# The first token block computed in two column halves, with the early transfers spread over other queues

## The chip, the cores and the metric

The kernel runs on one core of a Trainium2 chip. The metric is the device time of one execution in microseconds (us). The engines of a core work side by side, each through its own list of instructions in order, and wait for each other by semaphores: TensorE (PE in the profile; PEld is its weight load), VectorE (DVE), ScalarE (ACT), GpSimd (POOL) and SyncE (SP), which here only issues transfers. The two transfers' rings that matter are the hardware ring of SyncE and the software ring of GpSimd.

## The reference

Two layers, one behind the other: a causal convolution along the sequence, with one softmaxed filter of 7 taps for each of 8 heads of 24 channels, and a feed-forward layer with the exact GELU.

```python
# x: (8, 4096, 192) f32, weight: (8, 7)
w = softmax(weight, axis=-1)
x_pad = concat([zeros((B, 6, D)), x], axis=1)
x_unf = x_pad[:, idx, :].reshape(B, S, K, H, group)
y = einsum('hk,bskhg->bshg', w, x_unf).reshape(B * S, D)
# w_in: (192, 2048), w_out: (2048, 192), y: (32768, 192)
h = y @ w_in
g = 0.5 * h * (1.0 + erf(h / sqrt(2)))
return g @ w_out
```

## The kernel before

The 32768 tokens are two halves of 16384 that are worked on at the same time: one on partitions 0 to 63, the other on partitions 64 to 127. A half is cut into blocks n of WS[n] token columns, six of 256 and then 29 of 512. The 192 channels are three thirds p of 64. W_in's 2048 columns are 16 chunks of 128.

For each block the x load brings token rows into `xin` (four transfers, L252 to L265), VectorE transposes them into `xT`, a third at a time (`trans`, L465), GpSimd adds the six columns that come from the block before (`halo`, L344), the convolution gives `xc` in bf16, TensorE multiplies W_in with `xc` into PSUM (`mm1`, L659), ScalarE takes the GELU of 1024 columns a time into `gT` (L612), and TensorE multiplies with W_out (`mm2`, L693, for the blocks of 256 and the last one, `mm2_t`, L728, for the others). The results are evacuated and stored by SyncE.

The convolution of most blocks is done on VectorE (`conv`, L487: a tensor_scalar and six scalar_tensor_tensor a third). The first two blocks (`PC`, L34) have theirs on TensorE (`pconv`, L627): `xT` is cast to bf16 (`xTb`), and for each third and tap two 64x64 diagonal matrices `dg` (made by `diag`, L427, a third at a time) multiply shifted columns of it, 14 matmuls a third. The sum lands in one PSUM bank a third (`CONVB`, L166) and is copied to `xc`: for block 0 by ScalarE (cast at L572, copy at L579), for block 1 by VectorE (`cast`, L452, `conv_out`, L459).

TensorE's order at the start is: 16 warm-up matmuls (L625), the 42 convolution matmuls of block 0, then mm1(0,i) for the slices i = 0 to 7. A slice is two chunks by 256 columns, 12 matmuls, and fills one of the two PSUM buffers `hp`; slice i waits until GELU i-2 has emptied it. Behind slices 4, 5 and 6 comes one third each of block 1's convolution (`behind`, L655). Then mm1(1,0), and from there mm1(1,i) with pieces of mm2(0) between, the first of which waits for W_out (L782).

W_in comes in three parts (`win_in`, columns 0:256, 256:512, 512:1024 of each half, L322), and each partition half needs the other's columns too: VectorE copies them across (`dup`, L435, two copies a part). mm1(0,0), (0,2) and (0,4) wait for the parts 0, 1 and 2 and their copies (L669).

The order on VectorE at the start (L523 to L536) is diag(0), diag(1), trans(0,0..2), diag(2), dup(0..2), trans(1,0..2), cast(1,0..2), and then block 2's operations, with conv_out(1,0..2) put between them. GpSimd's (L379 to L390) is halo(0), six x loads (two of block 1, four of block 2, named in `SW`, L131), the W_out transfer, halo(1), four x loads of block 3, then the halos of the other blocks. SyncE has the first two loads of block 0, waits for W_in's first part, has the other two of block 1, waits for block 3's loads (L799), and goes on with block 4; ScalarE issues the other two loads of block 0.

Of the kernel before, what the change touches and what calls it, by code (L numbers as in the profile page):

```python
# [11 lines left out]
def bass_lightweight_conv__then__act_gelu_exact_kernel(  # L12
# [7 lines left out]
    B, SEQ, D = x.shape  # L20
# [12 lines left out]
    WS = [256] * 6 + [512] * ((HALF - 1536) // 512)  # L33
    PC = {0: 0, 1: 1}  # L34

    NA = 6
# [67 lines left out]
    with es:  # L104
# [24 lines left out]


        SW = {1: (2, 3), 2: (0, 2, 1, 3), 3: (0, 2, 1, 3)}  # L131

        S_WSB = sem("S_WSB")
        S_WIN = [sem("S_WIN%d" % i) for i in range(3)]
        S_WOUT = sem("S_WOUT")
        S_XG = {n: sem("S_XG%d" % n) for n in SW}
        S_XIN = [sem("S_XIN%d" % i) for i in range(NX)]
# [7 lines left out]
        S_HOT = sem("S_HOT")  # L145
        S_CAST = [sem("S_CAST%d" % i) for i in range(len(PC))]
        S_PC = sem("S_PC")
# [16 lines left out]


        CONVB = {0: [0, 1, 2], 1: [3, 0, 1]}  # L166

        NCV = NP * KS
# [7 lines left out]

        def pce(n, p):

            return NP * PC[n] + p + 1

# [9 lines left out]
        def xin_at(n):  # L190

            return sum(64 - 16 * len(SW.get(m, ())) for m in range(n % NX, n + 1, NX))

# [15 lines left out]
        def wait_banks(t, m, g):  # L209

            k = G0[m] + g
            if m < M0:
                if k >= 2:
                    t.wait_ge(S_EVA, k - 1)
            else:
                e = k - G0[M1]
                t.wait_ge(S_EV, EVC[M1] + (-2 if e == 0 else e - 1))

        def evac(e, m, g):
# [32 lines left out]
        def load(e, n, qs=(0, 2, 1, 3), sm=None):  # L252
            mb = WS[n] // 32
            if n >= NX:
                e.wait_ge(S_TR, NP * (n - NX + 1))
            for q in qs:
                off = ((q // 2) * HALF + OFF[n]) * D + DQ * (q % 2)
                e.dma_start(  # L258
                    ap(
                        xin[n % NX],  # L260
                        32 * q * (TB // 32 * DQ),
                        [[TB // 32 * DQ, 32], [DQ, mb], [1, DQ]],
                    ),
                    ap(xt, off, [[mb * D, 32], [D, mb], [1, DQ]]),
                ).then_inc(sm or S_XIN[n % NX], 16)  # L265
# [55 lines left out]
        def _(g):  # L321
# [22 lines left out]
            def halo(n):  # L344
# [3 lines left out]
                if n >= 2 and n not in PC:  # L348
                    if n - 2 in PC:
                        g.wait_ge(S_PCE, pce(n - 2, NP - 1))  # L350
                    else:
                        g.wait_ge(S_CV, cvd(n - 2))
# [27 lines left out]
            halo(0)  # L380
            load(g, 1, SW[1], S_XG[1])
            load(g, 2, SW[2], S_XG[2])
            g.dma_start(
# [3 lines left out]
            halo(1)  # L387
            load(g, 3, SW[3], S_XG[3])
            for n in range(2, NB):
# [3 lines left out]
        def _(v):  # L393
# [57 lines left out]

            def cast(n, p):  # L452
                v.wait_ge(S_TR, NP * n + p + 1)
                v.tensor_copy(
                    ap(xTb[PC[n]], p * XB + HL, [[NP * XB, 128], [1, WS[n]]]),
                    ap(xT[n % 2], p * XW + HL, [[NP * XW, 128], [1, WS[n]]]),
                ).then_inc(S_CAST[PC[n]])

            def conv_out(n, p):  # L459
                v.wait_ge(S_PC, pce(n, p))  # L460
                v.tensor_copy(  # L461
                    xc[n % 2][:, p * TB : p * TB + WS[n]], bank(CONVB[n][p], w=WS[n])
                ).then_inc(S_PCE)

            def trans(n, p):  # L465
                w = WS[n]
                if p == 0:
                    if xin_at(n) > 0:
                        v.wait_ge(S_XIN[n % NX], xin_at(n))
                    if n in SW:  # L470
                        v.wait_ge(S_XG[n], 16 * len(SW[n]))
                    if n >= 2 and n - 2 in PC:
                        v.wait_ge(S_PCE, pce(n - 2, NP - 1))
                    elif n >= 2:
                        v.wait_ge(S_CV, cvd(n - 2))
                    if n >= 1:
                        v.wait_ge(S_HALO, HC[n])
                v.transpose(  # L478
                    ap(xT[n % 2], p * XW + HL, [[NP * XW, 128], [1, w]]),
                    ap(  # L480
                        xin[n % NX],
                        p,
                        [[TB // 32 * DQ, 128], [DQ, w // 32], [NP, 32]],
                    ),
                ).then_inc(S_TR)
# [36 lines left out]

            diag(0)  # L523
            diag(1)
            for p in range(NP):
                trans(0, p)
            diag(2)
            dup(0)
            dup(1)
            dup(2)  # L530
            for p in range(NP):
                trans(1, p)
            for p in range(NP):
                cast(1, p)

            side = [((2, (0, 3, 5)[p]), conv_out, 1, p) for p in range(NP)]  # L536
            for n in range(M0, M1):
# [18 lines left out]
        def _(a):  # L556
# [12 lines left out]
            a.activation(out=hot[:, 1:2], in_=warm[0:1, 0:1], func=AF.Gelu).then_inc(S_HOT)  # L569
            for p in range(NP):  # L570
                a.wait_ge(S_TR, p + 1)
                a.activation(  # L572
                    out=ap(xTb[0], p * XB + HL, [[NP * XB, 128], [1, WS[0]]]),
                    in_=ap(xT[0], p * XW + HL, [[NP * XW, 128], [1, WS[0]]]),
                    func=AF.Copy,
                ).then_inc(S_CAST[0])
            for p in range(NP):
                a.wait_ge(S_PC, p + 1)
                a.activation(  # L579
                    out=xc[0][:, p * TB : p * TB + WS[0]],  # L580
                    in_=bank(CONVB[0][p], w=WS[0]),
                    func=AF.Copy,
                ).then_inc(S_PCE)

            due = {(1, 6): [(0, 0)]}
# [4 lines left out]
            for n in range(NB):  # L590
                w = WS[n]
                for i in range(NSL[n]):
# [5 lines left out]
                    if i == 0 and n >= 2:  # L598
                        a.wait_ge(S_MM2, MMC[n - 1])
                    if M0 <= n < M1:  # L600

# [6 lines left out]
                    else:  # L608
# [3 lines left out]
                    a.activation(  # L612
                        out=ap(gT[n % 2], i * c * 2 * w, dst),
                        in_=ap(hp[u % 2], 0, src),
# [7 lines left out]
        def _(t):  # L622
# [3 lines left out]

            def pconv(n, p, k):  # L627

                w = WS[n]
                if k == KS - 1:  # L630
                    t.wait_ge(S_CAST[PC[n]], p + 1)
                    if n == 0:
                        t.wait_ge(S_DG, p + 1)
                if k == KS - 2:
                    t.wait_ge(S_HALO, HC[n] + 2 + p)
                for hf in range(2):
                    r = slice(64 * hf, 64 * hf + 64)
                    d0 = (p * KS + k) * 64
                    x0 = p * XB + 32 * k
                    ins = t.matmul(  # L640
                        bank(CONVB[n][p], r, w),
                        dg[r, d0 : d0 + 64],
# [7 lines left out]

            taps = [(p, k) for p in range(NP) for k in range(KS - 1, -1, -1)]
            for p, k in taps:
                pconv(0, p, k)

            behind = {}  # L655
            for p in range(NP):
                behind[0, 4 + p] = [(1, p, k) for k in range(KS - 1, -1, -1)]

            def mm1(n, i):  # L659
                w, c = WS[n], NCH[n]  # L660
                u = SL0[n] + i
                if u >= 2:
                    t.wait_ge(S_GELU, u - 1)
                if i == 0:
                    if n in PC:
                        t.wait_ge(S_PCE, pce(n, NP - 2))
                    else:
                        t.wait_ge(S_CV, cvd(n))
                if n == 0 and i in (0, 2, 4):  # L669
                    t.wait_ge(S_WIN[i // 2], 32)  # L670
                    t.wait_ge(S_DUPE, 2 * (i // 2) + 2)
                for cc in range(c):
                    f0 = 128 * CH[i * c + cc]
                    for p in range(NP):
                        if n in PC and i == 0 and cc == 0 and p == NP - 1:
                            t.wait_ge(S_PCE, pce(n, p))
                        for hf in range(2):
                            r = slice(64 * hf, 64 * hf + 64)
                            fw = 64 if M0 < n <= M1 else 128
                            for fo in range(0, 128, fw):  # L680
# [4 lines left out]
                                    win[r, f1 : f1 + fw],  # L685
                                    xc[n % 2][r, p * TB : p * TB + w],
                                    start=(p == 0),
# [5 lines left out]
            def mm2(m, g, ph, i):  # L693
# [4 lines left out]
                if i == 0:  # L698
                    if ph == 0:
                        wait_banks(t, m, g)  # L700
                    else:
                        t.wait_ge(S_PH, PHC[m] + g + 1)
                if g == 0 and ph == 0:

                    c = NCH[m]
                    if i % max(c, 8) == 0:
                        last = min(NF, i + max(c, 8))
                        t.wait_ge(S_GELU, SL0[m] + last // c)
# [63 lines left out]
            for n in range(NB):  # L772
                todo = units(n - 1) if n >= 1 else []
                for i in range(NSL[n]):
                    mm1(n, i)
                    for q in behind.get((n, i), []):
                        pconv(*q)
# [16 lines left out]
        def _(sp):  # L794
            sp.dma_start(wsb[:, :], ap(wt, 0, [[KS, H], [1, KS]])).then_inc(S_WSB, 16)
            load(sp, 0, (0, 1))
            sp.wait_ge(S_WIN[0], 32)
            load(sp, 1, (0, 1))
            sp.wait_ge(S_XG[3], 64)  # L799
            for n in range(1, NB):  # L800
# [35 lines left out]
```

## Time and profile before

| | |
|---|---|
| time, median of 6 executions | 686.46 us (685.98 to 687.57) |
| the profiled execution | 685.98 us, of which the span from first to last instruction is 684.2 us |
| granted TensorE clock | 1.00 |
| matmuls mm1 (L683) | 6048, 418.6 us busy |
| matmuls mm2_t (L747) and mm2 (L714) | 5376, 366.4 us, and 1024, 52.2 us |
| convolution matmuls (L640) | 84, 5.3 us |
| GELU (L612) | 512, 1023 ns each |
| convolution on VectorE (L508, L501) | 594 and 99 instructions, 435.3 us |
| W_out transfer | issued by GpSimd at 12.22 us, 768 KB, 8.5 us to landing |

Busy times of TensorE overlap: two matmuls on different halves of the array run at once, so the sum of the groups is above the span. A line of the chain of waits says when a piece began, how long it held up the chain, and what it was; a line of the timeline gives start, length, engine, source line, operation, tiles and count, and in brackets what the engine idled for just before. All times start from the span's first instruction.

### The profile page before, as it was taken

Reading aid. Unit: us, or ns where it says so; the run is one execution under the profiler, and the core shown is the slowest. Engines: PE = TensorE matmul, PEld = TensorE weight load, DVE = VectorE, ACT = ScalarE, POOL = GpSimd, SP = SyncE. Lnnn points to the kernel's source line nnn. Section 1 sums busy time; section 2 is a strip of 40 time slices with the busy share of each in tenths; the row PEclk is TensorE's granted clock in tenths of the full one; section 3 lists DMA queues with packets and bytes.
Section 4 is the critical chain, followed back from the end, with each engine's and each line's share of the span. In section 5 each row is a group of like instructions: output and inputs, shape, how many; then the busy total and the mean of one; then the engine's idle time right before and its main releaser. Section 6 shows DMA issues by size and latency. Waiting matters only on the chain.

```text
span 684.2 us, 27314 instructions
## 1 busy us (share of the span) xinstructions
PE 677.5 (99%) x12548; PEld 409.2 (60%) x12548; DVE 580.6 (85%) x914; ACT 532.1 (78%) x536; POOL 45.6 (7%) x97
## 2 busy tenths in 40 slices
PE   8999999999999999999999999999999999999997
PEld 4899655555555555555555555555555555555556
DVE  7999989888899888898888898888898888998702
ACT  6788987777787777777877778777778777877771
POOL 8110000000000000000000000000000000000000
PEclk9999999999999999999999999999999999999999
DMA  8444521244432344422344422444323444221224
GB/s 137 93 110 97 116 61 36 61 95 95 94 69 50 74 94 95 94 53 56 84 94 95 87 53 53 93 94 94 72 56 65 95 94 95 59 56 30 48 49 94
DMA packets 133234, 53.66 MB, mean 78 GB/s; under 512 B 127552, under 2 KB 132960, under 8 KB 133120
## 3 DMA queue, kind: packets, MB, share of 16 engines
q1 hardware_dynamic: 128144, 48.78, 33.6%
q0 software_dynamic: 3792, 2.56, 2.5%
q8 instruction: 98, 1.61, 1.0%
q10 hardware_dynamic: 1184, 0.59, 0.3%
q14 instruction: 16, 0.13, 0.1%
HBM read 28.31 MB, written 25.17 MB: 78 GB/s over the span
## 4 chain that ended last, share of the span: by engine, by line
PE 96%; ACT 2%; DVE 1%; issue 0%; ACTq 0%
PE hp L683 47%; PE ob L747 42%; PE ob L714 5%; ACT gT L612 2%; PE ob L640 1%; DVE dg L428 0%; ACT L558 0%; ACT osb L227 0%; DVE wcol L420 0%; DVE osb L247 0%; DVE osb L229 0%; DVE xT L478 0%; ACT xTb L572 0%; ACT wex L562 0%; ACT xc L579 0%
## 5 line engine op out<-in xcount | busy, mean ns | idle before, releaser
L612 ACT ACTIVATE gT<-hp 128x1024 bf16<-128x1024 f32 x512 | 522.9, 1023 | 133.2 <-PE hp L683 130.0
L683 PE MATMUL hp<-xc,win 64*64 64x512 bf16 (+2 forms) x6048 | 418.6, 366 | 1.0 <-ACT gT L612 0.7
L747 PE MATMUL ob<-gT,wout 64*64 64x512 bf16 x5376 | 366.4, 376 | 0.0
L508 DVE SCALAR_TENSOR_TENSOR acc<-xT,wcol,acc 128x512 f32<-128x512 f32 (+1 forms) x495 | 314.2, 698 | 0.0
L683 PEld LDWEIGHTS hp<-xc,win 64*64 64x64 bf16 (+1 forms) x6048 | 187.8, 106 | 135.6 <-ACT gT L612 2.1
L747 PEld LDWEIGHTS ob<-gT,wout 64*64 64x64 bf16 x5376 | 172.2, 118 | 122.9
L247 DVE STREAM_TRANSPOSE osb<-ob 128x512 f32<-128x512 f32 x84 | 73.8, 881 | 86.9 <-PE ob L747 86.9
L478 DVE STREAM_TRANSPOSE xT<-xin 128x512 f32<-128x512 f32 (+1 forms) x105 | 78.3, 797 | 0.0
L508 DVE SCALAR_TENSOR_TENSOR xc<-xT,wcol,acc 128x512 bf16<-128x512 f32 (+1 forms) x99 | 65.0, 710 | 0.0
L374 POOL COPY xT<-xT 128x558 f32<-128x558 f32 x33 | 21.5, 652 | 578.9 <-DVE xT L478 578.9
L501 DVE TENSOR_SCALAR acc<-xT,wcol 128x512 f32<-128x512 f32 (+1 forms) x99 | 56.1, 618 | 1.1
L714 PE MATMUL ob<-wout,gT 64*128 64x192 bf16 x1024 | 52.2, 243 | 0.3
L714 PEld LDWEIGHTS ob<-wout,gT 64*128 64x128 bf16 x1024 | 43.6, 94 | 6.4 <-PE ob L714 0.6
L357 POOL COPY xT<-xT 128x18 f32<-128x18 f32 x30 | 11.6, 386 | 1.4 <-DVE xc L461 1.4
L229 DVE COPY osb<-ob 128x384 f32<-128x384 f32 x4 | 2.2, 557 | 7.8 <-PE ob L714 7.8
L625 PE MATMUL hp<-warm 128*128 128x512 bf16 x16 | 5.9, 547 | 1.3 <-DVE warm L394 1.3
L640 PE MATMUL ob<-xTb,dg 64*64 64x256 bf16 x84 | 5.3, 272 | 0.7 <-ACT xTb L572 0.7
L227 ACT ACTIVATE osb<-ob 128x384 f32<-128x384 f32 x12 | 5.8, 486 | 0.0
L258 POOL DMA_DIRECT2D xin<-in_x_dram x10 | 5.8, 587 | 0.0
L640 PEld LDWEIGHTS ob<-xTb,dg 64*64 64x64 bf16 x84 | 4.3, 107 | 1.8 <-ACT xTb L572 1.2
L625 PEld LDWEIGHTS hp<-warm 128*128 128x128 bf16 x16 | 2.0, 132 | 4.6 <-issue 3.0
L324 POOL DMA_DIRECT2D win<-in_moe_w_in_dram x6 | 3.9, 651 | 0.0
(32 smaller groups left out, 21.8 us busy)
## 6 DMA issues: line engine op xcount, KB each, us to landing
xin<-in_x_dram SPq DMA_DIRECT2D x116, 192.0 KB, 4.5
out_dram<-osb SPq DMA_DIRECT2D x112, 192.0 KB, 3.6
out_dram<-osb SPq DMA_DIRECT2D x56, 48.0 KB, 1.7
xin<-in_x_dram SPq DMA_DIRECT2D x12, 96.0 KB, 3.0
xin<-in_x_dram POOLq DMA_DIRECT2D x10, 96.0 KB, 2.9
wout<-in_moe_w_out_dram POOLq DMA_DIRECT2D x1, 768.0 KB, 8.5
win<-in_moe_w_in_dram POOLq DMA_DIRECT2D x4, 96.0 KB, 3.9
win<-in_moe_w_in_dram POOLq DMA_DIRECT2D x2, 192.0 KB, 5.2
```

The source lines that it names most:

```text
L247: v.transpose(ap(osb[m % 2], j, [[8 * C, 128], [C // 2, TB // 32], [NP, 32]]), bank(ring(m, j)),).then_inc(S_EV)
L357: g.tensor_copy(dst, ap(xT[(n - 1) % 2], WS[n - 1] + 31, [[NP * XW, 128], [XW, NP], [32, HB]],),).then_inc(S_HALO)
L374: g.tensor_copy(ap(t, 1, [[NP * tw, 128], [tw, NP], [32, HB], [1, 31]]), ap(t, WS[n], [[NP * tw, 128], [tw, NP], [32, HB], [1, 31]]),).the ...
L478: v.transpose(ap(xT[n % 2], p * XW + HL, [[NP * XW, 128], [1, w]]), ap(xin[n % NX], p, [[TB // 32 * DQ, 128], [DQ, w // 32], [NP, 32]],),) ...
L501: ins = v.tensor_scalar(a, src, wk, None, ALU.mult)
L508: ins = v.scalar_tensor_tensor(dst, src, wk, a, op0=ALU.mult, op1=ALU.add)
L612: a.activation(out=ap(gT[n % 2], i * c * 2 * w, dst), in_=ap(hp[u % 2], 0, src), func=AF.Gelu,).then_inc(S_GELU)
L625: t.matmul(hp[1][:, 0:512], warm[:, 0:128], warm[:, :])
L640: ins = t.matmul(bank(CONVB[n][p], r, w), dg[r, d0 : d0 + 64], xTb[PC[n]][r, x0 : x0 + w], start=(k == KS - 1), stop=(k == 0), tile_positi ...
L683: ins = t.matmul(hp[u % 2][fo : fo + fw, o : o + w], win[r, f1 : f1 + fw], xc[n % 2][r, p * TB : p * TB + w], start=(p == 0), stop=(p == N ...
L714: ins = t.matmul(bank(bb[sub], w=C), gT[m % 2][r, c0 : c0 + 128], wout[r, CH[i] * C : (CH[i] + 1) * C], start=(ph == 0 and i == 0), stop=( ...
L747: ins = t.matmul(bank(ring(m, j), slice(64 * h, 64 * h + 64), w), ap(wout, 64 * hf * NF * C + CH[i] * C + j, [[NF * C, 64], [NP, 64]],), g ...
```

## The change

Block 0's convolution becomes two parts of 128 columns each, and block 1's a third (`PARTS`: block, first column, width, PSUM banks). TensorE does part 0, mm1(0,0), part 1 (`behind[0]`), mm1(0,1) and so on. For block 0 the slices 0 to 3 cover the chunks 0 to 7 in another way: four chunks by 128 columns, 24 matmuls a slice, slices 0 and 1 for the first columns and 2 and 3 for the second; slices 4 to 7 stay as they were. So mm1(0,0) needs W_in's part 0 and its copies, mm1(0,1) part 1, mm1(0,4) part 2. ScalarE writes the GELU of slices 0 to 3 to matching places of `gT`.

```diff
+    PARTS = [(0, 0, 128, (0, 1, 2)), (0, 128, 128, (3, 0, 1)), (1, 0, 256, (2, 3, 0))]
...
+            behind = {
+                0: third(1, 0) + third(1, 1) + third(1, 2),
+                4: third(2, 0),
+                5: third(2, 1),
+                6: third(2, 2),
+            }
...
+                part = {(0, 0): 0, (0, 2): 1, (1, 0): 2}.get((n, i))
+                if part is not None:
+                    t.wait_ge(S_PCE, pce(part, NP - 2))
...
+                if n == 0 and i < 4:
+                    w, c = 128, 4
+                    x0, ci = i // 2 * w, i % 2 * c
+                if n == 0 and i in (0, 1, 4):
+                    k = min(i, 2)
+                    t.wait_ge(S_WIN[k], 32)
+                    t.wait_ge(S_DUPE, 2 * k + 2)
```

The casts of part 0 are ScalarE's, those of part 1 GpSimd's, those of part 2 VectorE's; the copies to `xc` are ScalarE's for part 0 and VectorE's for the others. The third diagonal matrix set, diag(2) on VectorE before, is made by ScalarE in seven pieces of 64 columns. VectorE's order:

```diff
             diag(0)
+            trans(0, 0)
             diag(1)
-            for p in range(NP):
-                trans(0, p)
-            diag(2)
+            trans(0, 1)
+            trans(0, 2)
             dup(0)
             dup(1)
+            for p in range(NP):
+                conv_out(1, p)
             dup(2)
             for p in range(NP):
                 trans(1, p)
             for p in range(NP):
-                cast(1, p)
+                cast(v, 2, p)
```

ScalarE's:

```diff
+            a.wait_ge(S_PRO, 10)
+            a.wait_ge(S_IDN, 2)
+            for k in range(KS):
+                d0 = ((NP - 1) * KS + k) * 64
+                c0 = (NP - 1) * 32 + k
+                a.activation(
+                    out=dg[:, d0 : d0 + 64],
+                    in_=idb[:, :],
+                    func=AF.Copy,
+                    scale=wcol[:, c0 : c0 + 1],
+                ).then_inc(S_DGA)
...
+            cast0(0)
+            cast0(1)
+            conv_out0(0)
+            cast0(2)
+            conv_out0(1)
+            conv_out0(2)
```

Block 0's x load takes one run of 1440 elements a partition (eight rows of 192 less the last half row) in place of eight runs of 96, and the transposes of block 0 step over the half rows that are not wanted. GpSimd issues no x loads any more; its W_out transfer comes right behind its three casts:

```diff
             halo(0)
-            load(g, 1, SW[1], S_XG[1])
-            load(g, 2, SW[2], S_XG[2])
+            for p in range(NP):
+                cast(g, 1, p)
             g.dma_start(
                 ap(wout, 0, [[NF * C, 128], [C, NF], [1, C]]),
                 ap(woutt, 0, [[C, 128], [128 * C, NF], [1, C]]),
             ).then_inc(S_WOUT, 16)
             halo(1)
-            load(g, 3, SW[3], S_XG[3])
...
             sp.wait_ge(S_WIN[0], 32)
-            load(sp, 1, (0, 1))
-            sp.wait_ge(S_XG[3], 64)
+            load(sp, 1)
+            sp.wait_ge(S_WIN[2], 32)
+            load(sp, 2)
+            sp.wait_ge(S_WOUT, 16)
+            load(sp, 3)
```

The first pass of mm2(0) waits for the GELU of its chunks in smaller steps:

```diff
-                if g == 0 and ph == 0:
+                if m == 0:
+                    if g == 0 and ph == 0 and (i == 0 or i >= 8) and i % 2 == 0:
+                        t.wait_ge(S_GELU, max(4, i // 2 + 1))
+                elif g == 0 and ph == 0:
```

## The prediction

> **What bounds the kernel now.** I read four views, in this order: the page's busy times and its chain, to see which engine sets the end; the chain of waits over the first 60 us, since all edits lie there; the timeline of VectorE over the same stretch, since three of the edits rearrange that queue; and the groups by shape for durations.
>
> The page first: each engine's busy time, then the chain's shares.
>
> ```profile
> PE 677.5 (99%) x12548; PEld 409.2 (60%) x12548; DVE 580.6 (85%) x914; ACT 532.1 (78%) x536; POOL 45.6 (7%) x97
> PE 96%; ACT 2%; DVE 1%; issue 0%; ACTq 0%
> ```
>
> TensorE (PE) is the whole chain but for 4%, about 27 us, nearly all before the first 15 us and after 669 us. So a change to the ramp is worth what it shifts the moment from which TensorE is never again idle, one for one. The chain of waits over the first 60 us (start, length, what) shows that moment:
>
> ```profile
> 5.68 1.16 DVE dg L428 x2
> 6.84 0.45 DVE xT L478
> 7.31 0.43 ACT xTb L572
> ...
> 7.78 2.50 PE ob L640 x42
> 10.30 0.39 ACT xc L579
> ...
> 10.74 0.63 PE hp L683 x8
> 11.40 1.94 ACT gT L612 x2
> 13.35 1.03 ACT gT L612
> ...
> 14.42 0.83 PE hp L683 x12
> 15.25 0.88 PE ob L640 x14
> 16.13 0.76 PE hp L683 x12
> ```
>
> Two filter matrices, a transpose, a cast, 42 convolution matmuls, a copy, then GELUs 0 to 2 set the pace; from mm1(0,4) at 14.42 all is PE. Some 670 us follow. So the question is when mm1(0,4), and the work right behind it, starts in the new order. VectorE's timeline in the same stretch (start, length; in brackets what it idled for):
>
> ```profile
> 8.63 3.66 DVE L439 COPY win<-win 64x768 bf16<-64x768 bf16 x6
> 12.34 1.35 DVE L478 STREAM_TRANSPOSE xT<-xin 128x256 f32<-128x256 f32 x3
> 13.61 1.29 DVE L454 CAST xTb<-xT 128x256 bf16<-128x256 f32 x3
> 16.18 0.42 DVE L461 CAST xc<-ob 128x256 bf16<-128x256 f32 x1 [1.28 <-PE ob L640]
> 19.46 0.42 DVE L461 CAST xc<-ob 128x256 bf16<-128x256 f32 x1 [0.50 <-PE ob L640]
> ```
>
> The block-1 cast begins at 13.61 and TensorE takes up block 1's convolution at 15.18: VectorE has only some 0.8 us in hand there (the first cast is done 0.75 after its start, at 14.36). After 19.46 VectorE runs without idling until past 92 us; its last pieces of block 6 (from 70.59, 2.06 long) end at 72.67, and TensorE's first matmul of block 6 starts at 73.24. That is a second near-critical chain with 0.57 us of slack: TensorE can't gain more than that unless VectorE's 19.46 moves too.
>
> **The change part by part.**
>
> *x load of block 0 and the third filter matrix.* The load has one run of 1440 elements a partition instead of 8 of 96. Before, its last piece landed at about 6.7, with VectorE's second diag ending at 6.84 anyway. New order on VectorE: diag(0) from 5.68, pitch 0.54 (start to start; half of 1.16, less overlap), so trans(0,0) can start at 6.22 if the load is there, diag(1) at 6.62, trans(0,1) at 7.16, trans(0,2) at 7.58, end 8.07. But ScalarE now does seven 128x64 pieces of the third matrix first, from 5.68. No row has the shape. Bounds: from below the columns alone (GELU 1023 ns for 1024 columns against 417 for a 256-column cast is 0.79 ns a column, 0.05 us a piece, 0.35 in all); from above the 8x7 exponential with a per-partition operand, 298 ns, plus 57 columns, 0.346 a piece, 2.4 in all. Successive GELUs start 0.10 sooner than the one before ends, so I take 0.346 - 0.10 = 0.25, 1.75 in all: cast 0 starts at 7.43 instead of 7.31, and 128 columns take 417 - 101 = 0.32. First convolution matmul: 7.78, as before. **The earlier x and the moved diag bring nothing there**; if the load lands as late as before, 0.06 is lost further on. The longer runs carry 0.34 MB more, beside W_in: at the 168 GB/s of the stretch from 10 to 20 us that is 2.0 us if W_in had to wait for all of it. Its three parts landed at 6.7, 8.8 and 10.8 and are now wanted at 8.1, 9.1 and 12.2; 2.0 late, the second would hold VectorE up by 1.7 and push dup(2) by some 0.5. The other bound is nothing, as the longer runs also need an eighth of the descriptors; I take nothing.
>
> *Half-width convolution, W_in halves.* The chain gives 16 matmuls of 192 columns in 0.66 us and 12 of 256 in 0.66, two running side by side: 82 and 109 ns a pair. The line through both gives 55.5 ns at 128 columns, 0.39 per third (seven pairs). No 128-column row exists: bounds 54.5 (half of 256) and 82 (the nearest row); I take the line, since the 512-column rows (216 ns) lie on it. Third p0 runs 7.78 to about 8.17, p1 straight on; ScalarE then evacuates p0 before it casts p2 (8.58 to 8.9), so p2 runs 8.94 to 9.33, its evacuation (0.28) ends 9.86, and mm1(0,0) has its last third at 9.9 instead of 10.74. Ten pairs are left, 0.56; GELU 0 starts near 10.65 instead of 11.40. **A lead of 0.75 us.**
>
> *Part 1 behind mm1(0,0).* 42 more matmuls, 21 pairs, 1.17 us, and two changes between 64x64 and 64x128 tiles. In the trace each such change makes the start-to-start gap 0.20 instead of 0.11, so 0.09 each. mm1(0,1) goes from about 10.4 + 1.17 + 0.18 to 11.78, its 12 pairs take 0.67, and GELU 1 starts at 12.67; ScalarE idled 1.0 for it. Before, GELU 1 was at 12.32. **The lead is gone, and 0.35 more.** GELU 2 then goes at 13.6 (13.35), mm1(0,4) at 14.65 to 14.7: 0.28 late.
>
> *VectorE.* It now waits for part 1's three thirds (evacuations of 0.29 to 0.30 us at 11.1, 11.5, 11.9) before dup(2), which had started at 10.79. dup(2) then runs 12.23 to 13.78 at its old 1.55, trans(1) follows at 13.78 instead of 12.34, the cast at 15.04 instead of 13.61, part 2's first third at 15.83 instead of 15.18: 0.65, some 0.7 with the gaps behind it. Against that, the old dup(2) ran while GpSimd issued transfers, and it won't now. The cast row shows what company costs: 277 ns for the last, 743 for the first, which ran beside GpSimd's copies. At three quarters of 1.55 the shift falls to 0.33, where mm1(0,4) decides anyway. I take the middle, **+0.5 us**. VectorE's chain of later blocks moves by the same, so its slack of 0.57 holds.
>
> *Queues.* GpSimd gives up ten x loads (0.58 each to issue) and takes three 128x128 casts after its halo copies; its 186-column cast takes 0.34, so about 0.3 each, 8.46 to 9.36; behind them in its queue stand the W_out transfer and halo(1). Part 1 needs them at 10.5 to 11.3, so they are free; at 1.0 each they would cost 0.23. W_out's issue comes at 9.4 instead of 12.22. It took 8.5 to land; even with 2.5 added for the eight x loads now beside it (at 0.6 to issue, four of them within its time), it lands by 20.4, and mm2 wants it at 20.74 + 0.5. Before, mm2 waited some 0.1 for it: that is all there is to gain. SyncE waits for the third W_in part (10.76) with load 2 behind it: issued to 13.2, landed at 15 to 16 by its 3.0; VectorE wants it at 17.1. Load 3 waits for W_out, lands near 23, wanted at 27. Covered by 1 to 4 us each. The finer waits of mm2(0) on GELU cost and win nothing: it begins at 20.7, after GELU 4 to 6, and reaches its eighth chunk after 22, when GELU 7 is done.
>
> [...]
>
> [...]
>
> The sum: 684.2 + 0.5 on the span, 685.98 + 0.5 = 686.5 for the profiled execution. That execution was the fastest of those shown; the median is 686.46, so I predict 687.0.
>
> **The rivals.**
>
> *The lead holds* (0.17). If the seven pieces cost near their lower bound, everything from cast 0 is up to 0.45 earlier: +0.26 with the old dup(2), -0.13 with the fast one. With all terms at their low ends, the VectorE waits gone too, perhaps -1.0: 685.5 to 686.6. For it: ScalarE is idle there today. Against: the cast then waits for VectorE's trans(0,1) at 7.67.
>
> *Narrow matmuls cost what the 192-column row costs* (0.15). 50 pairs lie on the chain between cast and GELU 1 (7 of the last third, 10, 21, 12); 27 ns more each is 1.35, so 688.4. It decides from about 73 ns a pair, where the total passes 1.37 us. For it: the row is the nearest. Against: its weight load, 94 ns, is already longer than its 82 ns pair and hides.
>
> *A transfer comes late* (0.13). The ring of SyncE now carries x beside W_out. If x of block 1 lands after 13.8, block 2 after 17.1 or W_out after 21.3, each us is a us: at two late, 689. For it: the x pieces that competed with W_in took 3.7 to 4.2 us to land. Against: the margins above.
>
> **How the numbers follow.** Forecast 0.55, 686.7 to 687.4. The range reaches to the lead that holds and to the narrow matmuls: 685.6 to 688.5. 0.2%, 1.37 us, is about what a measurement can tell from no change. Faster takes the far end of the first rival, 0.05; slower takes the second, most of the third and the slow end of the ScalarE pieces (2.4 in all gives +1.4), 0.25; the rest, 0.70, is the same.
>
> **What would show it.** Right: first convolution matmul at 7.8, GELU 0 near 10.65, ScalarE idle about 1 us before GELU 1 near 12.7, mm1(0,4) at 14.7, the block-1 cast on VectorE near 15, pairs of 128 columns at 55 ns, no TensorE wait at W_out. Wrong: GELU 1 before 12.3, part 2 of the convolution before 15.2, or any TensorE wait for W_out or an x load.

## The result and the profile after

The changed kernel takes 688.13 us (median of 18 runs, 687.77 to 692.47) against 686.80 for the kernel before (38 runs, 685.96 to 689.42). The ratio is 1.0025, 95% interval 1.0015 to 1.0036: **slower by about a quarter of a per cent**, where +0.5 us, less than a tenth of a per cent, was forecast. The time itself lies within the range given. The profiled execution has a span of 686.1 us, 1.9 more than the 684.2 before.

The page of the changed kernel: busy times of three engines, then the shares of its chain, then the group of VectorE's transposes (busy, mean ns; idle before them and what ended it), then W_out's transfer (size, us to landing).

```profile
PE 678.4 (99%) x12638; PEld 410.1 (60%) x12638; DVE 580.8 (85%) x916; ACT 533.2 (78%) x543; POOL 41.0 (6%) x90
...
PE 94%; DMA 2%; ACT 1%; DVE 1%; POOL 1%; issue 0%; SPq 0%
...
L475 DVE STREAM_TRANSPOSE xT<-xin 128x512 f32<-128x512 f32 (+1 forms) x105 | 78.3, 797 | 3.2 <-DMA xin<-in_x_dram 3.2
...
wout<-in_moe_w_out_dram POOLq DMA_DIRECT2D x1, 768.0 KB, 9.7
```

The work of TensorE, VectorE and ScalarE is the same to within 1.1 us. What is new is in the chain: DMA, absent from it before, has 2%, and in front of the transposes VectorE idled 3.2 us for x, where it hadn't idled at all before. The chain of waits of the changed kernel, from 5 to 23 us (start, length, what), says which load it is:

```profile
5.08 4.95 DMA win<-in_moe_w_in_dram
...
10.04 0.56 SPq L269
...
11.97 7.47 DMA xin<-in_x_dram
...
19.46 1.33 DVE xT L475 x3
20.80 0.30 DVE xc L460
21.10 0.61 DVE acc L498 x2
...
21.84 0.42 DVE xc L460
...
22.31 0.61 PE hp L722 x8
```

It reads backwards from TensorE's mm1(1,0) at 22.31: it needed a copy of block 1's convolution (`conv_out`, L460), which stood in VectorE's queue behind the transposes of block 2, which waited until 19.44 for the last piece of x block 2. That piece was issued at about 12 us, after SyncE had waited for W_in's third part (to 10.02), and took 7.47 us. The timeline of the changed kernel (start, length, engine; in brackets what the engine idled for) has the ramp in order:

```profile
5.29 1.78 ACT L574 ACTIVATE dg<-idb,wcol 128x64 bf16<-128x64 bf16 x7 [0.97 <-DVE wcol L425]
...
7.36 2.04 PE L667 MATMUL ob<-xTb,dg 64*64 64x128 bf16 x42 [0.25 <-ACT xTb L584]
...
9.55 1.20 POOL L389 DMA_DIRECT2D wout<-in_moe_w_out_dram  x1
10.44 1.36 PE L667 MATMUL ob<-xTb,dg 64*64 64x128 bf16 x42
10.55 1.02 ACT L636 ACTIVATE gT<-hp 128x1024 bf16<-128x1024 f32 x1 [0.83 <-PE hp L722]
...
12.62 3.90 ACT L636 ACTIVATE gT<-hp 128x1024 bf16<-128x1024 f32 x4 [1.04 <-PE hp L722]
...
14.88 0.84 DVE L219 CAST xTb<-xT 128x256 bf16<-128x256 f32 x3
...
15.37 0.95 PE L667 MATMUL ob<-xTb,dg 64*64 64x256 bf16 x14
...
19.46 1.33 DVE L475 STREAM_TRANSPOSE xT<-xin 128x256 f32<-128x256 f32 x3 [2.67 <-DMA xin<-in_x_dram]
19.54 0.83 PE L722 MATMUL hp<-xc,win 64*128 64x256 bf16 x12
...
21.25 0.40 PE L722 MATMUL hp<-xc,win 64*128 64x256 bf16 x4 [0.88 <-DVE xc L460]
...
22.31 0.61 PE L722 MATMUL hp<-xc,win 64*128 64x256 bf16 x8 [0.66 <-DVE xc L460]
...
23.25 0.82 PE L722 MATMUL hp<-xc,win 64*128 64x256 bf16 x12
```

The same places in the timeline of the kernel before are these: block 2's transposes, mm1(0,7) with mm1(1,0) in one group, and mm1(1,1).

```profile
16.52 1.33 DVE L478 STREAM_TRANSPOSE xT<-xin 128x256 f32<-128x256 f32 x3
...
19.35 1.49 PE L683 MATMUL hp<-xc,win 64*128 64x256 bf16 x24
...
21.30 0.83 PE L683 MATMUL hp<-xc,win 64*128 64x256 bf16 x12
```

The first point at which TensorE lags is the one to find. Its last slice of block 0, mm1(0,7), starts at 19.54, against 19.35 before: the whole rearranged ramp costs **0.19 us**. Then it stops twice, 0.88 and 0.66 us. mm1(1,1) starts at 23.25, against 21.30 before: 1.95 late, which is the 1.9 of the span (0.19 and 1.54 of the stops make 1.73; the stops are counted from the end of the group in front, and the overlap of successive groups, 0.17 at the first stop, is lost with them).

Why the load came late is seen in the transfers. The lines are of the view of the DMA engines from 9 to 24 us in 40 slices of 0.375 us, busy share in tenths and GB/s; the changed kernel first, then the kernel before.

```profile
DMA  9997474978999999999999999800000737574896
GB/s 238 263 166 170 77 188 80 76 48 82 162 184 197 193 195 193 195 197 198 196 197 196 196 197 197 129 6 0 0 0 9 163 102 183 125 131 66 215 205 109
```

```profile
DMA  9977949857942148999999999999996400010027
GB/s 196 275 173 190 214 152 248 203 156 167 202 127 44 5 13 47 81 128 181 193 188 189 168 180 196 193 202 327 295 302 157 80 22 0 0 44 0 0 68 194
```

Before, the engines ran empty around 14 us (slices 12 to 15): x of blocks 1 and 2 was in, and W_out then filled them alone. After, from slice 12 to 24 (13.5 to 18.4 us) they are full and pinned at 193 to 198 GB/s, with W_out and x block 2 in them together. Counted in the trace from 13.5 to 18.5 us, 0.5 us hold on the average ten W_out packets and five x packets an engine, all of 384 bytes. The packets of x block 2 ran from 12.58 to 18.58 us: 384 KB in 6.0 us, 66 GB/s, a third of what the engines moved. The pieces of x block 2 landed at 14.76, 16.99, 18.27 and 19.44; W_out landed at 19.22, after 9.7 us instead of 8.5.

### The profile page after: what moved, and what is told of

Read it like the earlier page. It is cut to its first block, busy times and chain, and to the rows that moved or that the text cites. A ratio compares the mean times of both kernels' runs of the same rounds, so it can differ in the third digit from the quotient of the medians.

```text
span 686.1 us, 27507 instructions
## 1 busy us (share of the span) xinstructions
PE 678.4 (99%) x12638; PEld 410.1 (60%) x12638; DVE 580.8 (85%) x916; ACT 533.2 (78%) x543; POOL 41.0 (6%) x90
## 4 chain that ended last, share of the span: by engine, by line
PE 94%; DMA 2%; ACT 1%; DVE 1%; POOL 1%; issue 0%; SPq 0%
PE hp L722 47%; PE ob L789 42%; PE ob L756 5%; ACT gT L636 1%; DMA xin<-in_x_dram 1%; DMA win<-in_moe_w_in_dram 1%; POOL win L330 0%; SPq L269 0%; DVE xT L475 0%; ACT osb L232 0%; DVE osb L252 0%; DVE xc L460 0%; DVE acc L498 0%; DVE osb L234 0%; POOL idb L338 0%
## 5 line engine op out<-in xcount | busy, mean ns | idle before, releaser
L722 PE MATMUL hp<-xc,win 64*64 64x512 bf16 (+3 forms) x6096 | 419.1, 364 | 2.3 <-DVE xc L460 1.5
L667 PE MATMUL ob<-xTb,dg 64*64 64x128 bf16 (+1 forms) x126 | 6.1, 237 | 0.4 <-ACT xTb L584 0.2
L444 DVE COPY win<-win 64x768 bf16<-64x768 bf16 (+1 forms) x6 | 3.9, 650 | 0.2
```

The costliest lines, as they stand in the source:

```text
L667: ins = t.matmul(bank(bk[p], r, w), dg[r, d0 : d0 + 64], xTb[PC[n]][r, x0 : x0 + w], start=(k == KS - 1), stop=(k == 0), tile_position=(64 ...
L722: ins = t.matmul(hp[u % 2][fo : fo + fw, o : o + w], win[r, f1 : f1 + fw], xc[n % 2][r, p * TB + x0 : p * TB + x0 + w], start=(p == 0), st ...
```

## The experiments

Times are medians, ratios are against the kernel before as run beside them (686.51 for the first four, 686.46 for the last two). Spans are of the profiled executions.

**1. x block 2 ahead of W_out.** The changed kernel, with the four loads of block 2 put into GpSimd's ring ahead of W_out (with a semaphore of their own). Everything else of the change stays, the halves too.

```diff
             for p in range(NP):
                 cast(g, 1, p)
+            load(g, 2, sm=S_XG)
             g.dma_start(
...
             load(sp, 1)
-            sp.wait_ge(S_WIN[2], 32)
-            load(sp, 2)
             sp.wait_ge(S_WOUT, 16)
```

> The changed kernel, but the four loads of x block 2 stand in GpSimd's queue ahead of the W_out transfer, as in the kernel before; SyncE does not issue them. All of the new arithmetic stays. Theory A (the loss is x block 2 landing at 19.44 us beside W_out, wanted at about 16.7): the block lands by about 14, VectorE takes it up at about 16.7, TensorE's two stops of 0.88 and 0.66 us before the second half of mm1(1,0) vanish, W_out lands at about 20.5 (wanted at about 20.9), span 684.4 us against 686.1, time within 0.1% of before. Theory B (the column halves cost the time: narrow matmuls, GELU 1 late): the span stays at 686 us, wherever x comes from. Theory C (W_out must start early for the new order): W_out at 20.5 or later makes TensorE stop at mm2 and gives back 0.5 us or more.

Measured: 686.67 us (686.43 to 687.02), ratio 0.9997 (0.9988 to 1.0005), span 684.8. x block 2 landed from 12.27 to 14.71 and W_out at 20.07. The timeline of this kernel:

```profile
11.70 1.20 POOL L391 DMA_DIRECT2D wout<-in_moe_w_out_dram  x1
...
12.21 1.92 DVE L446 COPY win<-win 64x1536 bf16<-64x1536 bf16 x2
...
17.07 1.32 DVE L479 STREAM_TRANSPOSE xT<-xin 128x256 f32<-128x256 f32 x3
...
19.91 1.48 PE L726 MATMUL hp<-xc,win 64*128 64x256 bf16 x24
...
21.23 0.66 PE L760 MATMUL ob<-wout,gT 64*128 64x192 bf16 x12
```

The transposes wait for nothing, mm1(0,7) and mm1(1,0) run through as one group of 24, and the loss of time is gone. So the place of one load in the queues carries the loss; W_out's issue, which stands behind it, came 2.15 us later than in the changed kernel, and the fourth experiment asks what that does alone. The span is 0.4 above what was expected. The trace has the place: with W_out's issue at 11.70 beside it, dup(2) took 1.92 instead of 1.40, so part 2's convolution and all behind it came some 0.4 later.

**2. The transfers alone.** The kernel before, with nothing but its queues changed, as the change has them: the x loads of blocks 1 to 3 in SyncE's ring with the new waits, W_out next in GpSimd's.

```diff
-        SW = {1: (2, 3), 2: (0, 2, 1, 3), 3: (0, 2, 1, 3)}
+        SW = {}
...
             halo(0)
-            load(g, 1, SW[1], S_XG[1])
-            load(g, 2, SW[2], S_XG[2])
             g.dma_start(
...
-            load(sp, 1, (0, 1))
-            sp.wait_ge(S_XG[3], 64)
+            load(sp, 1)
+            sp.wait_ge(S_WIN[2], 32)
+            load(sp, 2)
+            sp.wait_ge(S_WOUT, 16)
+            load(sp, 3)
```

> The kernel before, with nothing but the queues changed: all x loads of blocks 1 to 3 in SyncE's ring (block 2 behind the third W_in part, block 3 behind W_out), W_out next in GpSimd's. Theory A: x block 2 lands at about 19, VectorE idles some 2 us for it, and the whole loss is there without any column half: span 685.7 to 686.2 us against 684.2, 0.2 to 0.3% slower. Theory B: the span stays within 0.3 us of 684.2.

Measured: 690.15 us (688.0 to 691.25), ratio 1.004 (1.0025 to 1.0056), span 688.5: +4.3, more than twice what was expected. The compute part is as before (GELU 0 at 11.39, mm1(0,4) at 14.42); x block 2 landed from 17.43 to 20.16. The timeline:

```profile
20.18 1.32 DVE L475 STREAM_TRANSPOSE xT<-xin 128x256 f32<-128x256 f32 x3 [3.59 <-DMA xin<-in_x_dram]
...
21.96 0.40 PE L680 MATMUL hp<-xc,win 64*128 64x256 bf16 x4 [1.78 <-DVE xc L458]
...
23.02 0.61 PE L680 MATMUL hp<-xc,win 64*128 64x256 bf16 x8 [0.66 <-DVE xc L458]
...
24.06 1.49 PE L680 MATMUL hp<-xc,win 64*128 64x256 bf16 x12
```

The two stops are the changed kernel's, and longer: 2.44 us. The last line explains what is left. Twelve matmuls, 0.82 us elsewhere, take 1.49 while nothing is waited for. The same kernel in windows (window and length; busy time of the five engines with counts in brackets; PEclk; DMA share; GB/s) gives the reason in the column PEclk, the granted clock as a share of full speed:

```profile
20.00:23.00 3.00, 0.57 (x8) 0.14 (x4) 2.82 (x8) 1.02 (x1) 0.65 (x1) 1.00 0.42 100
23.00:24.00 1.00, 0.98 (x20) 0.94 (x22) 1.00 (x4) 0.33 (x1) 0.27 (x1) 0.92 0.76 169
24.00:27.00 3.00, 3.00 (x36) 2.53 (x34) 3.00 (x9) 1.72 (x2) 0.00 (x0) 0.50 0.52 109
27.00:28.00 1.00, 0.94 (x18) 0.57 (x13) 1.00 (x4) 0.20 (x1) 0.00 (x0) 0.87 0.03 6
```

TensorE was busy for 0.57 of the 3 us up to 23. Right behind that its granted clock fell to 0.50 and stayed there for about 3.4 us (0.16 in the second window, 3.0, and 0.26 in the fourth). That costs 0.08 + 1.50 + 0.13 = 1.71 us. With the stops it makes 4.15 of the 4.3. So the late load was right as the cause of the loss, and its size was missed because the two stops, 2.44 us themselves, had the fall of the clock behind them, 1.71 us more. One execution of the six ran at a mean clock of 1.00, with a span of 686.3, 2.1 above before, close to the stops alone; the other five had 0.997 to 0.998 and spans of 687.9 to 689.5. In the profiled execution of the changed kernel TensorE was busy 1.46 us from 20 to 23 and the clock stayed at 1.00; five of its executions had 0.997 or 0.998, and those are its upper times, 689.55 to 692.47.

**3. The copies first.** The changed kernel, with the three copies of block 1's convolution put ahead of block 2's transposes on VectorE. The late load then no longer stands before what TensorE needs at mm1(1,0).

```diff
-            side = [((2, (0, 3, 5)[p]), conv_out, 2, p) for p in range(NP)]
+            side = [((2, 0), conv_out, 2, p) for p in range(NP)]
```

> The changed kernel, but on VectorE the three copies of block 1's convolution (part 2) stand ahead of block 2's transposes, so that nothing TensorE wants stands behind the late x. Theory A with the second chain (VectorE's own work up to block 6 has only 0.57 us of slack): TensorE's stops at 21 to 22 us vanish, mm1(1,1) comes back to about 21.5, but block 2's transposes still start at about 19.5 to 20.1, so TensorE waits about 1.5 us for VectorE at block 6 (near 75 us) instead and the span is 685.8 to 686.2. Theory D (the loss is only the order of the copies behind the transposes): span 684.5, no stop at block 6.

Measured: 688.21 us (687.94 to 691.9), ratio 1.0026 (1.0011 to 1.0041), span 686.1: as slow as the changed kernel. TensorE's stops at 21 and 22 us are gone. The timeline has another in their place:

```profile
19.48 0.42 DVE L460 CAST xc<-ob 128x256 bf16<-128x256 f32 x1 [1.22 <-PE ob L667]
19.82 1.33 DVE L475 STREAM_TRANSPOSE xT<-xin 128x256 f32<-128x256 f32 x3
...
75.13 0.82 PE L722 MATMUL hp<-xc,win 64*128 64x512 bf16 x6 [1.70 <-DVE xc L505]
```

TensorE caught up with VectorE at block 6 and waited 1.70 us there. The transposes still began late (19.82 instead of 16.52), VectorE never idles again before block 6, and so its whole chain was late by more than the 0.57 us of slack it has there. So lateness has two ways to the end, and closing the first can hand it to the second. But the run doesn't show that it was the late load's: x block 2 landed at 19.62, and the third copy, now ahead of the transposes, waited for TensorE until 19.48 and kept VectorE to 19.82 in any case. Theory D, which had no stop at block 6, fell.

**4. W_out a little later.** The changed kernel, with GpSimd waiting for x block 1 before it issues W_out. Block 2's loads stay in SyncE's ring.

```diff
                 cast(g, 1, p)
+            g.wait_ge(S_XIN[1], 64)
             g.dma_start(
```

> The changed kernel, with GpSimd's W_out transfer held back until x block 1 has landed (12.25 us), 2.7 us later than now. Theory A (the two share the transfer engines and W_out's head start crowds x block 2 out): x block 2 lands at 15 to 17 instead of 19.44, W_out at 20.5 to 21.5, TensorE's stops fall from 1.54 to under 0.6 us, span 684.5 to 685.3. Theory E (SyncE's own issue of block 2, not the sharing, makes it late): the block lands at 19 as now and W_out later than now, span 686 or more.

Measured: 687.54 us (686.5 to 690.14), ratio 1.0013 (1.0001 to 1.0024), span 685.3. x block 2 landed from 13.09 to 17.98 and W_out at 21.93, both somewhat later than expected, and the span is at the far end of what theory A allowed. From the view of waits of this kernel (waited for: total, times, longest):

```profile
DVE xT L476 <- DMA xin<-in_x_dram: 1.3, 2, 0.8
...
PE ob L757 <- DMA wout<-in_moe_w_out_dram: 0.5, 1, 0.5
```

About half of the loss comes back by the medians, though this interval and the changed kernel's overlap. Both transfers are late now, x by 0.8 and W_out by 0.5. The 0.8 is a wait of VectorE alone; TensorE doesn't stop for a copy any more. What is left is the 0.5 at W_out and a ramp that is 0.57 late at mm1(0,7) (19.92 against 19.35), behind a copy of dup(2) that took 1346 ns beside W_out's issue in place of 686. So a later W_out alone only moves the lateness, from x to W_out; one behind the other, as in the first experiment, both come in time.

**5. Without the halves.** The first experiment's kernel, with block 0's convolution whole again: slices 0 to 3 as before, no casts on GpSimd, no copies of part 1 on VectorE. The third filter matrix stays on ScalarE, and the loads are where the first experiment has them.

```diff
-    PARTS = [(0, 0, 128, (0, 1, 2)), (0, 128, 128, (3, 0, 1)), (1, 0, 256, (2, 3, 0))]
+    PARTS = [(0, 0, 256, (0, 1, 2)), (1, 0, 256, (3, 0, 1))]
...
-            for p in range(NP):
-                conv_out(1, p)
             dup(2)
...
             behind = {
-                0: third(1, 0) + third(1, 1) + third(1, 2),
-                4: third(2, 0),
-                5: third(2, 1),
-                6: third(2, 2),
+                4: third(1, 0),
+                5: third(1, 1),
+                6: third(1, 2),
             }
```

> The kernel of x2_before_wout with the column halves taken out: block 0's convolution and mm1(0,0..3) at 256 columns again, block 1's cast on VectorE, no copies of part 1 on VectorE before the third W_in copy; it keeps the long x runs of block 0, the third filter matrix on ScalarE, x block 1 in SyncE's ring and x block 2 and then W_out in GpSimd's. Theory F (the halves themselves cost: part 1 stands between mm1(0,0) and mm1(0,1), and VectorE's third W_in copy waits for it): first convolution matmul near 7.4 us, GELU 0 near 11.0, GELU 1 at 11.9 to 12.0 against 12.66, mm1(0,4) near 14.1 against 14.65, span 683.7 to 684.0, 0.8 to 1.1 us below x2_before_wout and 0.2 to 0.5 below before. Theory G (the halves win and something else costs): GELU 1 no earlier than 12.6, span 684.8 or more.

Measured: 686.33 us (686.15 to 686.62), ratio 1.0 (0.9991 to 1.0008), span 684.4; 683.7 to 684.0 had been expected. The timeline:

```profile
7.65 2.83 PE L662 MATMUL ob<-xTb,dg 64*64 64x256 bf16 x42 [0.79 <-ACT xTb L584]
...
11.62 4.92 ACT L631 ACTIVATE gT<-hp 128x1024 bf16<-128x1024 f32 x5 [0.71 <-PE hp L713]
...
13.74 1.35 DVE L477 STREAM_TRANSPOSE xT<-xin 128x256 f32<-128x256 f32 x3 [1.81 <-DMA xin<-in_x_dram]
14.64 0.83 PE L713 MATMUL hp<-xc,win 64*128 64x256 bf16 x12 [0.21 <-ACT gT L631]
```

GELU 0 starts 1.0 us later than with the halves (11.62 against 10.60), and mm1(0,4) comes at 14.64, about where the halves have it (14.62 in the changed kernel), since GELUs 0 to 4 now run without a break. So the lead of the halves at GELU 0 buys nothing three GELUs later. Nor is it shown that they cost anything: the spans differ by 0.4, the two intervals overlap. Neither theory's numbers came: GELU 1 is at 12.54, between the two, and so is the span. The miss against theory F, 0.6 at GELU 0, has two places. The first matmul came at 7.65 instead of 7.4, behind an x that landed at 6.61. And the 42 matmuls took 2.83 us instead of 2.48: ScalarE's second cast waited 0.52 us for a transpose that now stands behind diag(1), and its third stands behind a copy. Block 1's x came late too, at 13.72, with VectorE idle for 1.81, but the convolution that needs it starts at 15.40, right behind mm1(0,4).

**6. The long runs alone.** The kernel before, with nothing changed but block 0's x load (one run of 1440 elements a partition) and the step of its transposes.

```diff
+                if n == 0:
+                    dst = [[TB // 32 * DQ, 32], [1, mb * D - DQ]]
+                    src = [[mb * D, 32], [1, mb * D - DQ]]
...
-                        [[TB // 32 * DQ, 128], [DQ, w // 32], [NP, 32]],
+                        [[TB // 32 * DQ, 128], [D if n == 0 else DQ, w // 32], [NP, 32]],
```

> The kernel before, with nothing changed but block 0's x load (one run of 1440 elements a partition) and the step of its transposes. Theory H (fewer runs are issued faster: ScalarE's two issues take 0.88 instead of 1.34 us, its exponential and all of VectorE's filter chain come 0.3 to 0.4 earlier): first filter matrix at 5.3 instead of 5.68, first convolution matmul at 7.4 to 7.5 instead of 7.78, span 683.8 to 684.0; W_out at 20.7 may take back some of it at mm2. Theory I (x or W_in land later for the 0.34 MB more): the transposes start at 6.7 or later, span 684.2 or more.

Measured: 685.88 us (685.57 to 686.42), ratio 0.9989 (0.998 to 0.9998), span 683.8. This is **faster than both kernels**, by little; the interval ends just below 1. The timeline:

```profile
1.25 0.89 ACTq L263 DMA_DIRECT2D xin<-in_x_dram  x2
...
5.29 1.16 DVE L428 TENSOR_TENSOR dg<-idb,wcol 128x448 bf16<-128x448 bf16 x2
...
7.38 2.48 PE L640 MATMUL ob<-xTb,dg 64*64 64x256 bf16 x42 [0.41 <-ACT xTb L572]
...
14.02 0.83 PE L683 MATMUL hp<-xc,win 64*128 64x256 bf16 x12 [0.20 <-ACT gT L612]
...
20.38 0.67 PE L714 MATMUL ob<-wout,gT 64*128 64x192 bf16 x12
```

ScalarE's two x issues, ahead of the softmax in its queue, take 0.89 us instead of 1.34. The softmax and with it the first filter matrix come at 5.29 instead of 5.68, and the lead of 0.40 lasts to mm1(0,4) (14.42 before) and to mm2 (20.74). The span fell by the same 0.4. The load also landed earlier, at 6.21 instead of 6.74, and that was needed too: the transposes start at 6.37. The kernel of the first experiment has the long runs as well, and its span is 684.8: against this run, what is left of the change costs about 1.0 us.

## Why the prediction was wrong

**The step that failed** lies in the part on the queues: "SyncE waits for the third W_in part (10.76) with load 2 behind it: issued to 13.2, landed at 15 to 16 by its 3.0; VectorE wants it at 17.1", with its conclusion "Covered by 1 to 4 us each". The issue times were nearly right (10.04 to 13.14, for 10.76 to 13.2). The landing wasn't: 14.76 to 19.44. The 3.0 is the median of the twelve loads of 96 KB that SyncE issues in the kernel before, none of which ran beside W_out; this one did. The same paragraph had charged W_out 2.5 us for that company and charged x nothing. It was the wrong way round: W_out, 768 KB, lost 1.2 us, and the last piece of x took 7.47. The rate of 66 GB/s is known only from this trace. But an estimate from half of the 190 GB/s that W_out moves alone in the trace of before gives 384 KB 4.1 us. With the 2.5 us that this trace shows from the first issue to the first packet, and the 0.9 from the last packet to the landing, that is 18.3 from an issue at 10.76, past the 17.1 at which it was wanted.

The trace shows the two transfers mixed: both queues' packets stand in every 0.5 us from 12.58 us to 18.58, some 196 GB/s in all. What the trace calls a packet is a run of 384 bytes here, and it doesn't show the order on one engine. The shares weren't fixed: from 14.0 to 14.5 us x had 1.1 packets an engine to W_out's 14.5, and from 17.5 to 18.0 it had 7.9 to W_out's 8.1; in the second experiment x had no packet at all from 13.09 to 14.84 us, and from 17.0 to 17.5 it had 15 an engine to W_out's 5.

**The rival that came true** is "A transfer comes late". It set the point from which block 2's load decides at 17.1 and the price at a us for each us; at 19.44 that gives 2.3, and 1.7 to 1.8 were lost. It had 0.13, with the argument against it that the margins were large, and the margins were the numbers that were wrong.

**The likeliest case, point by point.** The forecast's sum for the ramp was +0.5; it measured +0.19. That it came so near is in part luck, since the sum lacks a gain of 0.4.

- *ScalarE's filter pieces:* 1.75 for seven, measured 1.78. Right.
- *First convolution matmul:* 7.8, measured 7.36. The x load was seen only as a transfer that might land sooner. It landed at 6.42, against 6.74 before, and what counts is the issue: it lets the filter matrices start 0.39 earlier through ScalarE's queue, as the sixth experiment shows by itself. This term was left out of the sum.
- *Half-width matmuls:* 55.5 ns a pair. Measured, the pairs of mm1(0,1) and mm1(0,2) start 56 ns apart in the trace. The rival of the narrow matmuls, which decides from about 73, fell.
- *GELU 0 and GELU 1:* 10.65 and 12.67, measured 10.55 and 12.62; ScalarE idled 1.04 us in front of GELU 1, where 1.0 was worked out. The loss behind part 1 came as forecast, and so the rival "The lead holds" fell. The lead at GELU 0 came by luck: the convolution began 0.42 earlier than forecast, and 0.3 of that was lost between its thirds. The first waited for GpSimd's first halo cast, which took 0.64 us, and the second for a cast that had itself waited 0.63 for VectorE. Against the sixth experiment, which has the long runs alone and GELU 0 at 11.00, the lead is 0.45, and mm1(0,4) is 0.60 late (14.62 against 14.02).
- *mm1(0,4):* 14.65 to 14.7, measured 14.62.
- *VectorE:* cast at 15.04, measured 14.88; part 2 at 15.83, measured 15.37. dup(2) took 1.40, between the two bounds. Part 2 stands right behind mm1(0,4) again (14.62 and 0.75), so that mm1(0,4) decides: of the two cases, 0.33 and 0.65, between which the sum took the middle, it was the lower, and mm1(0,4) itself was less late, 0.20 where 0.28 was forecast.
- *Moving W_out:* worth 0.1 at most by the row of mm2's wait. The first experiment, with W_out's issue at 11.70, and the changed kernel, with 9.55, both show no wait of TensorE for it. There was nothing to buy with the early start.
- *VectorE's slack at block 6:* 0.57, named as a second chain and then judged safe. The third experiment shows it deciding when the transposes come late.

So two errors of opposite sign met in the sum: a ramp priced 0.3 too high, for want of the issue's 0.4, and a load priced 1.7 to 1.8 too low. What moved the verdict to slower is the load, as the first experiment shows.

## What to carry to other kernels

A transfer's landing time from a quiet stretch is no price for a busy one (3.0 us there, up to 7.47 beside W_out here): ask which transfers share the engines in that stretch, and charge the small one for the large one, not only the reverse. Moving up a load that hardly anything waited for, W_out here, had 0.1 us to win and cost more than that; if such a load must move, put it behind the loads that are wanted first, in the same ring, as in the first experiment (span 684.8 for 686.1). And where a second engine has half a us of slack for the next fifty (0.57 here, and a stop of 1.70 in the third experiment), a reordering of its queue has to be priced there too.

## What the runs showed of the hardware

- **Behind two stops the granted clock fell to half.** In the second experiment TensorE worked 0.57 us of the 3 up to 23, and from 23.85 on it ran at 0.50 for about 3.4 us. Not every stop had that behind it: in the changed kernel, where TensorE worked 1.46 us of the same 3, and in the third experiment, with a stop of 1.70 us at 73 us, the clock stayed at 1.00. How much idling it takes is not shown.
- **The shape of block 0's load was paid by the engine that issued it.** One run a partition instead of eight took two issues on ScalarE from 1.34 to 0.89 us. ScalarE had work on the critical path behind them here, and that work came 0.39 earlier.
- **One of VectorE's copies took longer beside W_out's issue on GpSimd.** dup(2) took 1.40 us without it and 1.92 with it (first experiment); one copy of dup(1) took 1059 ns beside it in the changed kernel and 533 before, where an x load was being issued. Three more runs have one such copy, of 1060 to 1346 ns. Each time it is a copy that began 0.3 to 0.5 us after the issue; in the fifth experiment a copy of dup(2) began 0.05 us before the issue and took 687 ns. What the two engines share there is not shown.
